# Sparse attention feeding a two-layer network: the scores of two head pairs in one visit to half-height products

## The chip, the cores and the metric

The kernel runs on one core of one Trainium2 chip. The metric is device time in microseconds (us), the median of several executions. The core has TensorE (PE, with its weight loads as PEld), VectorE (DVE), ScalarE (ACT), GpSimd (POOL) and SyncE (SP, here only a queue of DMAs). TensorE writes to PSUM[...].

## The reference

Eight batches (b) of eight heads, 576 positions, head size 64. Heads 0 to 3 see the last 32 positions, heads 4 to 7 the earlier positions of the same residue modulo 32. Then a two-layer network on all 4608 positions, with 512 inputs, 2048 hidden units and a PReLU between.

```python
scores = scale * np.matmul(q, k.transpose(0, 1, 3, 2))
mask_local = (rel >= 0) & (rel < 32)
mask_strided = (rel >= 0) & (pos[None, :] % 32 == pos[:, None] % 32)
attn = softmax(np.where(mask, scores, -1e9))          # local for heads 0-3, strided for 4-7
x = np.matmul(attn, v).transpose(0, 2, 1, 3).reshape(4608, 512)
h = x @ w_in
out = (np.maximum(h, 0.0) + alpha * np.minimum(h, 0.0)) @ w_out
```

## The kernel before, in words

**Network.** It works in nine blocks n of 512 positions, each in 30 steps i. Steps 0 to 15 are the first layer (`lin1_piece`): one step makes 128 hidden units for 512 positions with four products of 512 columns (line L678; eight of 256 in block 4, whose positions wrap in the ring `xT`) into one of three PSUM banks hb0 to hb2, handed out in turn by `hbank()`. ACT makes `neg` from the bank (L697), then DVE makes `gT` from `neg` and the bank (L700), which frees the bank. Steps 16 to 29 are the second layer (`lin2_sums`): seven products of half-size matrices in place of eight, two steps each, eight products of 256 columns a step (L811), into three accumulators A, B and C in the same three banks. The seven products need sums of parts of `gT` (`g_sum`, L760): on POOL at steps 5, 9 and 13, the rest on DVE at steps 16, 18 and 20. Accumulator C is written first at step 26.

**Attention.** It is cut into pieces that stand in one list, and each step of the network takes its share (`attn_n`, `attn_step`), so that block n carries batch n+1. A head pair is g = 4b + hp; hp 0 and 1 are local, 2 and 3 strided. Two pairs make a unit u = g // 2. The pieces of a pair are:

- Scores ("S", `score_both`). For each of 6 groups of 96 queries (local) or 8 groups of 72 (strided) and each of two heads y, a product of half height: the 64 rows of head y, rows 0-63 or 64-127 of the array, so that two heads' products stand side by side. A visit is one such run of products. The first half of the pair's groups goes to a two-bank PSUM tile `sp`, the other half to two tiles `sph` of the `ps` pool. ACT takes the exponential into an SBUF tile `et` (one for `sp`, L464; one for each `sph`, L474), and POOL multiplies with the mask (L468, L470, L477). The exps of the `sph` tiles wait in a list `defer`, of which each `attn_step` runs one.
- Attention times v ("P", `pv_piece`): products of 65 columns into a `ps` tile `pv` (L512; six products, or four in the third piece of a strided pair, PV(4) below), then a reciprocal (L521) and a multiply (L523) on DVE, which free it.
- Transposes of the result into `xT`: by DMA on SP (`x_dma`, with `x_copy` on ACT), or for hp 3 on PE ("X", `xp`).

The `ps` pool has three one-bank buffers, used in rotation by `sph`, `pv`, `xp` and the transposed inputs. Every engine works in the order written (`keep`); `late` puts L700 behind PE's next piece. POOL's queue also issues loads (`load_d`, `load_v`, `load_l`), SP's the transposing DMAs (`transpose_d`, `transpose_l`) and the stores.

The order of the pieces is:

```python
if okA:
    seq.append(("S", lambda a=a: score_both(pairs[a])))
if okP:
    seq.append(("P", Pv(p, 0)))
...
if 8 <= g - 2 < npair and not pairs[g - 2].xd:
    seq.append(("X", X(g - 2)))
if okP:
    seq.append(("P", Pv(p, 1)))
```

Of the kernel before, what the change touches and what calls it, by code (L numbers as in the profile page):

```python
# [9 lines left out]
F32 = mybir.dt.float32  # L10
# [22 lines left out]
def kernel(  # L33
# [10 lines left out]
    nc = tc.nc  # L44
# [56 lines left out]
    vss = [cpool.tile([128, 4, 8, 65], F16, name=f"vs{i}") for i in range(2)]  # L101
    ets = [cpool.tile([128, 800], F16, name=f"et{i}") for i in range(NE)]
    x16s = cpool.tile([80, 1024], F16)
# [57 lines left out]
    def cast_s(b, nm, eng):  # L161
        t16 = hpool.tile([128, 2, 512], F16, tag=f"{nm}s", bufs=2, name=f"{nm}s")
# [77 lines left out]
    def make_pair(g):  # L240
# [14 lines left out]
        P.pgroups = ([0, 1, 2], [3, 4, 5], [6, 7]) if P.strided else P.sgroups  # L255
        if P.lx:
            P.sgroups = ([0, 1, 2, 3], [4, 5])
        P.et = {}
# [163 lines left out]

    defer, defer_et = [], {}
    late = []
    second = {"on": False}

    def score_both(P):

        w, r = P.w, 72 if P.strided else 128
        for i in range(2):  # L430
# [9 lines left out]
            for x, t in enumerate(grp):  # L440
                if P.dx:
                    q0 = k0 = 80 * (4 * (2 * P.pr + t % 2) + t // 2)
                elif P.lx:
                    j = 3 * (2 * P.pr + t % 2) + t // 2
                    q0, k0 = 96 * j, 128 * j
                else:
                    q0, k0 = w * t, 32 + 72 * t if P.strided else 96 * t
                for y in range(2):
# [4 lines left out]
                        skip_group_check=True))  # L453
                    P.et[(2 * (t // 2) + y, t % 2) if P.dx or P.lx else (t, y)] = (et, n * y + w * x)
            ev = et[0:r, 0 : 2 * n]
            if not P.strided and i == 0 and not P.lx:
                mv = ev.rearrange("r (y c) -> r y c", y=2)
                m = mfirst.unsqueeze(1).to_broadcast([r, 2, n])
            else:
                z = 2 * w if P.lx and i == 0 else 0  # L460
                mv = ev[:, z:].rearrange("r (c f) -> r c f", f=w)
                m = (mstr if P.strided else mother).unsqueeze(1).to_broadcast([r, (2 * n - z) // w, w])
            if i == 0:
                keep(nc.scalar.activation(  # L464
                    ev.rearrange("r (y c) -> r y c", y=2), sp[0:r, :, 0:n], AF.Exp, scale=SCALE))
                if P.lx:
                    fv = ev[:, 0 : 2 * w].rearrange("r (c f) -> r c f", f=w)
                    keep(nc.gpsimd.tensor_tensor(  # L468
                        fv, fv, mfirst[:, 0:96].unsqueeze(1).to_broadcast([r, 2, w]), op=ALU.mult))
                keep(nc.gpsimd.tensor_tensor(mv, mv, m, op=ALU.mult))  # L470
                continue
# [6 lines left out]

            defer_et["et"] = et
            if second["on"]:  # L480
                ex(0)
                defer.append(lambda: ex(1))
            else:
                defer.extend([lambda: ex(0), lambda: ex(1)])

    def pv_piece(P, a):
        run_masks(P)
        while defer and any(P.et[z][0] is defer_et["et"] for z in P.et):
            defer.pop(0)()
        if P.x16 is None:  # L490
# [86 lines left out]
    for g in range(7, npair + 2):  # L577
# [6 lines left out]
        seq = []  # L584
        if okA:
            seq.append(("S", lambda a=a: score_both(pairs[a])))
# [66 lines left out]
    def attn_step(end):  # L653
# [6 lines left out]
        if defer:  # L660
            defer.pop(0)()

# [98 lines left out]

    lay, held = {}, {}

# [214 lines left out]
    for m in (2, 1, 0, *range(3, 16)):  # L978
# [97 lines left out]
```

## Time and profile before

| what | value |
|---|---|
| median of 3 runs | 300.24 us (299.53 to 300.42) |
| the profiled execution | 300.0 us, of which the span 298.1 us |
| PE, DVE, ACT, POOL busy in the span | 289.9, 227.8, 173.5, 168.5 us |
| blocks 3, 4 and 5, from first layer to first layer | 122.8 to 153.0, to 183.3, to 213.5 us: 30.2 each |
| in block 5 (183.3 to 213.5): PE, DVE, ACT, POOL busy | 30.1, 23.6, 18.2, 20.0 us |
| L678, a product of 512 columns | 0.379 us from start to end, one every 0.216 |
| L811, a product of 256 columns | 0.273 us, one every 0.109 |
| L697 on ACT, L700 on DVE | 0.597 and 0.744 us |
| granted clock | 1.0 throughout |

A row of the timeline has the start in us from the span's start, the duration of the row, engine, line, operation, output and inputs, the shapes, how many instructions are merged in it, and in brackets how long the engine was idle before it and what ended the wait. A PE row ends with its last result, some 0.16 us after the next product can start.

### The profile page before, as it was taken

Reading aid. Unit: us, or ns where it says so; the run is one execution under the profiler, and the core shown is the slowest. Engines: PE = TensorE matmul, PEld = TensorE weight load, DVE = VectorE, ACT = ScalarE, POOL = GpSimd, SP = SyncE. Lnnn points to the kernel's source line nnn. Section 1 sums busy time; section 2 is a strip of 40 time slices with the busy share of each in tenths; the row PEclk is TensorE's granted clock in tenths of the full one; section 3 lists DMA queues with packets and bytes.
Section 4 is the critical chain, followed back from the end, with each engine's and each line's share of the span. In section 5 each row is a group of like instructions: output and inputs, shape, how many; then the busy total and the mean of one; then the engine's idle time right before and its main releaser. Section 6 shows DMA issues by size and latency. Waiting matters only on the chain.

```text
span 298.1 us, 7107 instructions
## 1 busy us (share of the span) xinstructions
PE 289.9 (97%) x2808; PEld 193.6 (65%) x2808; DVE 227.8 (76%) x427; ACT 173.5 (58%) x325; POOL 168.5 (57%) x182
## 2 busy tenths in 40 slices
PE   7899998999999999999999999999999999999995
PEld 3664445644886478646898887468746864784584
DVE  5788868979975988488848894889488858946872
ACT  3566556888557773776377636763676257406620
POOL 8952289359757996777777778665555003101300
PEclk9999999999999999999999999999999999999999
DMA  7999999995998969999999999993811140022004
GB/s 219 204 202 207 205 238 266 170 175 178 177 154 186 111 100 127 173 192 160 132 209 177 138 141 182 184 144 54 201 22 21 24 141 0 2 71 73 0 2 141
DMA packets 102273, 41.01 MB, mean 138 GB/s; under 512 B 80720, under 2 KB 99424, under 8 KB 102240
## 3 DMA queue, kind: packets, MB, share of 16 engines
q0 software_dynamic: 56336, 19.25, 61.1%
q1 hardware_dynamic: 45632, 20.78, 35.3%
q10 hardware_dynamic: 272, 0.52, 0.6%
q8 instruction: 22, 0.36, 0.6%
q14 instruction: 11, 0.09, 0.1%
HBM read 38.60 MB, written 9.44 MB: 161 GB/s over the span
## 4 chain that ended last, share of the span: by engine, by line
PE 80%; DMA 11%; POOL 4%; issue 2%; DVE 2%; ACT 1%; POOLq 0%
PE hb L678 36%; PE hb L811 32%; DMA ks<-in_k_dram 6%; PE pv L512 4%; DMA win<-in_moe_w_in_dram 3%; PE sp L450 2%; DMA ql<-in_q_dram 2%; PE hb L715 2%; PE opl L811 1%; PE xp L533 1%; PE tp L280 1%; DVE gT L700 1%; PE sph L450 1%; POOL ql L217 1%; POOL vl L205 0%
## 5 line engine op out<-in xcount | busy, mean ns | idle before, releaser
L678 PE MATMUL hb<-xT,win 128*128 128x512 f16 (+1 forms) x616 | 127.2, 357 | 0.0
L700 DVE SCALAR_TENSOR_TENSOR gT<-neg,oma,hb 128x512 f16<-128x512 f32 x138 | 100.7, 744 | 33.0 <-ACT neg L697 26.3
L697 ACT ACTIVATE neg<-hb 128x512 f32<-128x512 f32 x138 | 82.1, 597 | 32.7 <-PE hb L678 31.5
L678 PEld LDWEIGHTS <-win 128*128 128x128 f16 x640 | 60.0, 98 | 53.8
L760 POOL TENSOR_TENSOR gsum<-gT 128x512 f16<-128x512 f16 x23 | 26.5, 1152 | 68.9 <-DVE gT L700 68.9
L811 PEld LDWEIGHTS <-gsum 128*128 128x128 f16 x512 | 47.3, 98 | 6.0 <-DVE gsum L760 0.5
L811 PEld LDWEIGHTS <-gT 128*128 128x128 f16 x384 | 35.9, 98 | 6.0 <-issue 0.5
L470 POOL TENSOR_TENSOR et<-et,mmul 128x576 f16<-128x576 f16 (+1 forms) x24 | 30.6, 1274 | 14.6 <-issue 7.8
L823 ACT COPY o<-hb 128x512 f32<-128x512 f32 (+1 forms) x32 | 18.1, 569 | 32.5 <-PE hb L811 32.5
L523 DVE TENSOR_TENSOR x<-pv,rc 96x384 f16<-96x384 f32 (+2 forms) x65 | 34.5, 531 | 2.2
L811 PE MATMUL hb<-wout,gT 128*128 128x256 f16 x248 | 30.8, 273 | 0.1
L811 PE MATMUL hb<-wout,gsum 128*128 128x256 f16 x248 | 30.5, 272 | 0.0
L811 PE MATMUL hb<-wsum,gsum 128*128 128x256 f16 x248 | 30.3, 273 | 0.0
L477 POOL TENSOR_TENSOR et<-et,mmul 72x576 f16<-72x576 f16 (+2 forms) x24 | 29.3, 1220 | 0.4 <-ACT et L474 0.4
L826 DVE TENSOR_TENSOR o<-hb,o 128x512 f32<-128x512 f32 (+1 forms) x24 | 16.3, 681 | 17.0 <-PE hb L811 12.5
L464 ACT ACTIVATE et<-sp 72x576 f16<-72x576 f32 (+2 forms) x24 | 16.4, 685 | 20.6 <-PE sph L450 17.2
L512 PEld LDWEIGHTS <-et 72*128 72x128 f16 (+1 forms) x416 | 21.9, 98 | 8.0 <-issue 1.3
L474 ACT ACTIVATE et<-sph 72x288 f16<-72x288 f32 (+2 forms) x48 | 17.8, 388 | 0.0
L521 DVE RECIPROCAL rc<-pv 72x6 f32<-72x6 f32 (+2 forms) x80 | 14.5, 181 | 2.9 <-PE pv L512 2.4
L715 PE MATMUL hb<-wout,gT 128*128 128x512 f16 x64 | 15.6, 379 | 0.2 <-ACT osb L720 0.2
L811 PE MATMUL hb<-wsum,gT 128*128 128x256 f16 x120 | 15.3, 273 | 0.0
L760 DVE TENSOR_TENSOR gsum<-gT 128x512 f16<-128x512 f16 (+2 forms) x17 | 14.7, 865 | 0.2
(117 smaller groups left out, 318.0 us busy)
## 6 DMA issues: line engine op xcount, KB each, us to landing
out_dram<-o SPq DMA_DIRECT2D x31, 256.0 KB, 3.1
stv<-in_v_dram POOLq DMA_DIRECT2D x8, 288.0 KB, 8.4
vl<-in_v_dram POOLq DMA_DIRECT2D x6, 384.0 KB, 9.3
wout<-in_moe_w_out_dram POOLq DMA_DIRECT2D x4, 512.0 KB, 16.9
qsd<-in_q_dram POOLq DMA_DIRECT2D x6, 288.0 KB, 7.6
ksd<-in_k_dram POOLq DMA_DIRECT2D x6, 288.0 KB, 7.1
kl<-in_k_dram SPq DMA_DIRECT2D x3, 512.0 KB, 5.1
ql<-in_q_dram POOLq DMA_DIRECT2D x3, 512.0 KB, 6.4
```

The source lines that it names most:

```text
L470: keep(nc.gpsimd.tensor_tensor(mv, mv, m, op=ALU.mult))
L474: keep(nc.scalar.activation(ev[:, n * y : n * y + n], sps[y][0:r, 0:n], AF.Exp, scale=SCALE))
L477: keep(nc.gpsimd.tensor_tensor(mv, mv, m, op=ALU.mult))
L512: keep(nc.tensor.matmul(pv[:, 65 * x : 65 * x + 65], et[0:r, c : c + 128], v16[0:r, 2 * P.pr + hh, t, :] if P.strided else v16[:, 6 * (2 * ...
L523: keep(nc.vector.tensor_tensor(P.x16[0:w, c0 : c0 + 64 * nb].rearrange("r (c e) -> r c e", e=64), pvv[:, :, 0:64], rc[0:w, 0:nb].unsqueeze ...
L678: keep(nc.tensor.matmul(hps[:, dst : dst + w], win16[:, kk, 128 * m : 128 * m + 128], xT[:, kk, src : src + w], start=(first and kk == kks ...
L697: keep(nc.scalar.activation(neg, hps, AF.Relu, scale=-1.0))
L700: keep(nc.vector.scalar_tensor_tensor(gTs[n][:, m, :], neg, oma[:, m : m + 1], hps, op0=ALU.mult, op1=ALU.add))
L715: keep(nc.tensor.matmul(ops, gTs[n][:, kf, 128 * mt : 128 * mt + 128], wout16[:, kf, :], start=(kf == 0), stop=(kf == 15)))
L760: keep(eng.tensor_tensor(o[:, k0:k1], x[:, k0:k1], y[:, k0:k1], op=op))
L811: keep(nc.tensor.matmul(dst, lhs[:, kf, 128 * mt : 128 * mt + 128], rhs[:, kf, :], start=(first and own and kf == 0), stop=(kf == 7), skip ...
L823: keep(nc.scalar.copy(o, x))
```

## The change

From g = 16 on (batch 4) the first pair of a unit makes the scores of both pairs in one visit (`score_unit`), with the same products in another order. For each head y one stream runs through: the first pair's groups but the last one or ones, into `sp`; the leftover groups of both pairs, into c3 (y = 0, a `ps` tile) or c4 (y = 1); the second pair's groups, into c1 or c2 (`ps` tiles). c4 is an hb bank: the next in turn in the first layer, accumulator C's in the second. The exps of c4 and `sp` run in the visit; that of c3 does too in the second layer, and is first in `defer` in the first layer; c1 and c2 follow in `defer`. The results lie in `evs` (two tiles e1 and e2 for each of two units) and in `ets` for the leftovers (e3), and the masks are cut differently. The visit of a strided unit stands after the first PV piece of its slot, that of a local unit after the second; empty pieces "N" hold a place in the list and issue nothing of their own. The first batches' casts of strided q and k lie in `evs` now.

```diff
+    evs = [[cpool.tile([128, 1088], F16, name=f"ev{i}{j}") for j in range(2)] for i in range(2)]
...
-            t16 = hpool.tile([128, 2, 512], F16, tag=f"{nm}s", bufs=2, name=f"{nm}s")
+            t16 = evs[b]["qk".index(nm)][:, 0:1024].rearrange("p (f c) -> p f c", f=2)
...
+    def score_unit(u):
+        A, Bp = pairs[2 * u], pairs[2 * u + 1]
+        w, r, nb = A.w, 72 if A.strided else 128, 7 if A.strided else 5
+        n = nb * w
+        (e1, e2), e3 = evs[u % 2], ets[u % 2]
+        sp = pbpool.tile([128, 2, 512], F32, tag="sp", name="sp")
+        c3, c1, c2 = [pspool.tile([128, 512], F32, tag="ps", name="sph") for _ in range(3)]
+        c4 = lay["Cf"] if second["on"] else hbank()
+        rest = [(A, nb), (Bp, nb)]
+        streams = [
+            [(A, s, sp[:, 0], w * s) for s in range(nb)]
+            + [(P, s, c3, w * z) for z, (P, s) in enumerate(rest)]
+            + [(Bp, s, c1, w * s) for s in range(nb)],
+            [(A, s, sp[:, 1], w * s) for s in range(nb)]
+            + [(P, s, c4, w * z) for z, (P, s) in enumerate(rest)]
+            + [(Bp, s, c2, w * s) for s in range(nb)],
+        ]
+        for x in range(2 * nb + 2):
+            for y in range(2):
+                P, s, o, c = streams[y][x]
...
+                keep(nc.tensor.matmul(
+                    o[:, c : c + w], P.kT[hf, k0 : k0 + 128], P.qT[hf, q0 : q0 + w],
+                    start=(c == 0), stop=(c == (1 if s == nb else nb - 1) * w), skip_group_check=True))
...
+        def ex3():
+            ev = e3[0:r, 0 : 4 * w]
+            ex(ev[:, 0 : 2 * w], c3[0:r, 0 : 2 * w])
+            mask(ev.rearrange("r (c f) -> r c f", f=w),
+                 (mstr if A.strided else mother).unsqueeze(1).to_broadcast([r, 4, w]))
+        def ex2():
+            ex(e2[0:r, n : 2 * n], c2[0:r, 0:n])
+            masks(e2)
+        ex(e3[0:r, 2 * w : 4 * w], c4[0:r, 0 : 2 * w])
+        ex(e1[0:r, 0 : 2 * n].rearrange("r (y c) -> r y c", y=2), sp[0:r, :, 0:n])
+        masks(e1)
+        if second["on"]:
+            ex3()
+        else:
+            defer.append(((e3,), ex3))
+        defer.append(((e2,), lambda: ex(e2[0:r, 0:n], c1[0:r, 0:n])))
+        defer.append(((e2,), ex2))
...
+        units = g >= 4 * (DX + 2)
+        visit = okA and units and a % 2 == 0
-        if okA:
+        if okA and not units:
             seq.append(("S", lambda a=a: score_both(pairs[a])))
...
+        if visit and g % 4 == 2:
+            seq.append(("S", lambda a=a: score_unit(a // 2)))
+            seq.append(("N", lambda: None))
         if okP:
             seq.append(("P", Pv(p, 1)))
+        if visit and g % 4 == 0:
+            seq.append(("N", lambda: None))
+            seq.append(("S", lambda a=a: score_unit(a // 2)))
+            seq.append(("N", lambda: None))
...
-            for t in ets:
-                keep(nc.gpsimd.memset(t[:, 640:800], 0.0))
+            for t in evs[0] + evs[1]:
+                keep(nc.gpsimd.memset(t[:, 1024:1088], 0.0))
```

More of the change, by code (lines that the diff above doesn't have):

```diff
@@ L101 @@
     vss = [cpool.tile([128, 4, 8, 65], F16, name=f"vs{i}") for i in range(2)]
-    ets = [cpool.tile([128, 800], F16, name=f"et{i}") for i in range(NE)]
+    ets = [cpool.tile([128, 640], F16, name=f"et{i}") for i in range(NE)]
+    evs = [[cpool.tile([128, 1088], F16, name=f"ev{i}{j}") for j in range(2)] for i in range(2)]
     x16s = cpool.tile([80, 1024], F16)
@@ L161, in cast_s @@
     def cast_s(b, nm, eng):
-        t16 = hpool.tile([128, 2, 512], F16, tag=f"{nm}s", bufs=2, name=f"{nm}s")
+        t16 = evs[b]["qk".index(nm)][:, 0:1024].rearrange("p (f c) -> p f c", f=2)
         if eng[0] == eng[1]:
@@ L255, in make_pair @@
         P.pgroups = ([0, 1, 2], [3, 4, 5], [6, 7]) if P.strided else P.sgroups
-        if P.lx:
-            P.sgroups = ([0, 1, 2, 3], [4, 5])
         P.et = {}
@@ L421, in score_piece, with mask, masks, ex @@
         keep(nc.gpsimd.tensor_tensor(ev, ev, m, op=ALU.mult))
-    defer, defer_et = [], {}
+    defer = []
     late = []
+    lay = {}
     second = {"on": False}
+    def score_unit(u):
[18 more added lines that the diff above has]
+                P, s, o, c = streams[y][x]
+                if P.dx:
+                    q0 = k0 = 80 * (4 * (2 * P.pr + s % 2) + s // 2)
+                elif P.lx:
+                    j = 3 * (2 * P.pr + s % 2) + s // 2
+                    q0, k0 = 96 * j, 128 * j
+                else:
+                    q0, k0 = w * s, 96 * s
+                hf = slice(64 * y, 64 * y + 64)
+                keep(nc.tensor.matmul(
+                    o[:, c : c + w], P.kT[hf, k0 : k0 + 128], P.qT[hf, q0 : q0 + w],
+                    start=(c == 0), stop=(c == (1 if s == nb else nb - 1) * w), skip_group_check=True))
+                key = (2 * (s // 2) + y, s % 2) if P.dx or P.lx else (s, y)
+                P.et[key] = (e3, 2 * w * y + c) if s == nb else (e1 if P is A else e2, n * y + c)
+        def mask(v, m):
+            keep(nc.gpsimd.tensor_tensor(v, v, m, op=ALU.mult))
+        def masks(e):
+            ev = e[0:r, 0 : 2 * n]
+            if A.lx:
+                fv = ev[:, 0 : 2 * w].rearrange("r (c f) -> r c f", f=w)
+                mask(fv, mfirst[:, 0:96].unsqueeze(1).to_broadcast([r, 2, w]))
+                fv = ev[:, 2 * w :].rearrange("r (c f) -> r c f", f=w)
+                mask(fv, mother.unsqueeze(1).to_broadcast([r, 2 * nb - 2, w]))
+                return
+            k = 4 if A.strided else 3
+            fv = ev.rearrange("r (y c) -> r y c", y=2)
+            if A.strided:
+                m = mstr
+                for lo, hi in ((0, k), (k, nb)):
+                    mask(fv[:, :, w * lo : w * hi].rearrange("r y (c f) -> r y c f", f=w),
+                         m.unsqueeze(1).unsqueeze(1).to_broadcast([r, 2, hi - lo, w]))
+            else:
+                mask(fv[:, :, 0 : w * k], mfirst.unsqueeze(1).to_broadcast([r, 2, w * k]))
+                mask(fv[:, :, w * k :].rearrange("r y (c f) -> r y c f", f=w),
+                     mother.unsqueeze(1).unsqueeze(1).to_broadcast([r, 2, nb - k, w]))
+        def ex(o, i):
+            keep(nc.scalar.activation(o, i, AF.Exp, scale=SCALE))
+        def ex3():
[11 more added lines that the diff above has]
+            ex3()
+        else:
+            defer.append(((e3,), ex3))
+        defer.append(((e2,), lambda: ex(e2[0:r, 0:n], c1[0:r, 0:n])))
+        defer.append(((e2,), ex2))
@@ L442, in score_both @@
                     q0 = k0 = 80 * (4 * (2 * P.pr + t % 2) + t // 2)
-                elif P.lx:
-                    j = 3 * (2 * P.pr + t % 2) + t // 2
-                    q0, k0 = 96 * j, 128 * j
                 else:
@@ L453, in score_both @@
                         skip_group_check=True))
-                    P.et[(2 * (t // 2) + y, t % 2) if P.dx or P.lx else (t, y)] = (et, n * y + w * x)
+                    P.et[(2 * (t // 2) + y, t % 2) if P.dx else (t, y)] = (et, n * y + w * x)
             ev = et[0:r, 0 : 2 * n]
-            if not P.strided and i == 0 and not P.lx:
+            if not P.strided and i == 0:
                 mv = ev.rearrange("r (y c) -> r y c", y=2)
@@ L459, in score_both @@
             else:
-                z = 2 * w if P.lx and i == 0 else 0
-                mv = ev[:, z:].rearrange("r (c f) -> r c f", f=w)
-                m = (mstr if P.strided else mother).unsqueeze(1).to_broadcast([r, (2 * n - z) // w, w])
+                mv = ev.rearrange("r (c f) -> r c f", f=w)
+                m = (mstr if P.strided else mother).unsqueeze(1).to_broadcast([r, 2 * n // w, w])
             if i == 0:
@@ L465, in score_both @@
                     ev.rearrange("r (y c) -> r y c", y=2), sp[0:r, :, 0:n], AF.Exp, scale=SCALE))
[L466 to L469, printed above, removed]
                 keep(nc.gpsimd.tensor_tensor(mv, mv, m, op=ALU.mult))
@@ L477, in ex @@
                     keep(nc.gpsimd.tensor_tensor(mv, mv, m, op=ALU.mult))
-            defer_et["et"] = et
             if second["on"]:
                 ex(0)
-                defer.append(lambda: ex(1))
             else:
-                defer.extend([lambda: ex(0), lambda: ex(1)])
+                defer.append(((et,), lambda: ex(0)))
+            defer.append(((et,), lambda: ex(1)))
     def pv_piece(P, a):
         run_masks(P)
-        while defer and any(P.et[z][0] is defer_et["et"] for z in P.et):
-            defer.pop(0)()
+        used = [P.et[t, y][0] for t in P.pgroups[a] for y in range(2)]
+        while any(e is z for es, _ in defer for e in es for z in used):
+            defer.pop(0)[1]()
         if P.x16 is None:
@@ L660, in attn_step @@
         if defer:
-            defer.pop(0)()
+            defer.pop(0)[1]()
     gTs = {}
@@ L760, in g_sum @@
         keep(eng.tensor_tensor(o[:, k0:k1], x[:, k0:k1], y[:, k0:k1], op=op))
-    lay, held = {}, {}
+    held = {}
     def store(n, i, j, osb, mts=(0, 1)):
```

## The prediction

> **What bounds the kernel now.** First the page: busy shares, then the chain of waits.
>
> ```profile
> PE 289.9 (97%) x2808; PEld 193.6 (65%) x2808; DVE 227.8 (76%) x427; ACT 173.5 (58%) x325; POOL 168.5 (57%) x182
> ...
> PE 80%; DMA 11%; POOL 4%; issue 2%; DVE 2%; ACT 1%; POOLq 0%
> ```
>
> PE is the bound and the chain runs along it, so in the changed stretch (blocks 2 to 6, about 105 to 240 us) what PE saves or waits for counts one to one. The question is where PE leaves its own pace. The timeline of block 5's first layer:
>
> ```profile
> 186.07 2.75 PE L678 MATMUL hb<-xT,win 128*128 128x512 f16 x12
> ...
> 187.44 0.18 DVE L521 RECIPROCAL rc<-pv 96x6 f32<-96x6 f32 x1
> 187.66 0.55 DVE L523 TENSOR_TENSOR x<-pv,rc 96x384 f16<-96x384 f32 x1
> ...
> 188.13 2.10 DVE L700 SCALAR_TENSOR_TENSOR gT<-neg,oma,hb 128x512 f16<-128x512 f32 x3
> ...
> 188.76 0.30 PE L450 MATMUL sp<-qT,kT 64*128 64x72 f16 x8
> ...
> 188.89 0.29 PE L450 MATMUL sph<-qT,kT 64*128 64x72 f16 x8
> ...
> 189.12 2.76 PE L678 MATMUL hb<-xT,win 128*128 128x512 f16 x12
> ```
>
> *The visit.* Twelve products of 0.216 from 186.07 should end at 188.66; the first score product starts 0.10 later. Four pairs take 0.13 (sp to sph), so eight take 0.26, but L678 returns 0.36 after the start: another 0.10. A visit costs 0.46 us, 0.20 of it fixed.
>
> *The bank.* Step 3 starts at 186.07; PE takes 1.03 to its last result (L678 x4 at 225.72), ACT's neg 0.60, DVE's L700 0.745, hand-overs some 0.12: 2.50 us until its hb bank is free. Three steps of 0.865 are 2.60. So a bank comes back 0.1 us early if DVE and ACT are idle. DVE isn't after a PV piece: reciprocal and multiply put 0.69 (187.44 to 188.13) ahead of the next L700. Step 3's L700 ended at 188.87 (188.13 + 0.745), and only the score visit made the next user of its bank wait until 189.12.
>
> The second layer of the same block:
>
> ```profile
> 201.74 1.91 PE L811 MATMUL hb<-wsum,gsum 128*128 128x256 f16 x16
> ...
> 203.16 1.21 DVE L760 TENSOR_TENSOR gsum<-gT,gsum 128x2048 f16<-128x2048 f16 x1
> 203.58 0.28 PEld L450 LDWEIGHTS <-kT 64*128 64x128 f16 x12 [0.21 <-issue]
> 203.58 0.34 PE L450 MATMUL sp<-qT,kT 64*128 64x96 f16 x8
> 203.76 0.25 PE L450 MATMUL sph<-qT,kT 64*128 64x96 f16 x4
> 203.94 0.77 PEld L811 LDWEIGHTS <-gsum 128*128 128x128 f16 x8
> 203.94 1.05 PE L811 MATMUL hb<-wsum,gsum 128*128 128x256 f16 x8
> ...
> 204.50 0.42 DVE L523 TENSOR_TENSOR x16s<-pv,rc 72x256 f16<-72x256 f32 x1
> ...
> 205.07 0.34 PE L512 MATMUL pv<-vs,et 72*128 72x65 f16 x6
> ```
>
> Eight products of 0.109 from 203.94 end at 204.82, but PV starts at 205.07: 0.24 lost. Two sph tiles and the last pv tile fill the ps pool's three buffers; the oldest is free when L523 ends at 204.92, and PE starts 0.15 later. DVE was late because L760 (1.21) stood ahead. The same gap follows the score visits at 143.1 and 173.4.
>
> **What the skill says.** "TensorEngine Tiling (Array Packing)", Key Properties: changing the tiling mode drains TensorE. The trace agrees: 0.10 us at each edge of a visit. "TensorE: Matmul & The Clock Gate", Part 3, The mechanism: tiles in different row groups overlap. Agrees: a pair of 72-column products takes 33 ns, one 65-column PV product 30. "Perfetto Trace Analysis", Optimization Strategy: a gap that repeats can mean too few PSUM buffers. Agrees: the 0.24 us above. Same page, Optimizing Scalar/DVE Operations: half of an instruction's profiled latency can overlap the next. Here part of it does: starts stand 0.08 to 0.11 closer than durations, so I use such pitches (neg 0.49, L700 0.70).
>
> **The change, part by part.** The order of the changed program's instructions, step by step in blocks 3 to 5: steps 0-2, PV, 3-5, PV, 6-7, visit, 8-12, PV, 13-15, PV; second layer 1 step, PV, 2, PV(4), 1, PV, 1, PV, 3, visit, 2, PV(4), 2, PV, 1, xp, 1. The one visit per layer serves two pairs. I lay block 5's measured times on this order.
>
> 1. *Visits.* PE's score products stay the same in number and size; sixteen visits become eight. Saved: 8 x 0.21 = **-1.7**.
>
> 2. *The old ps wait.* PV no longer follows the visit with only one step between. Saved: 3 x 0.24 = **-0.7**.
>
> 3. *First layer, steps 6 and 8.* PV now stands where the first visit stood (0.18 for 0.46), so step 6 comes at 188.85 and its bank at 188.92: 0.07. That second PV puts its 0.69 ahead of step 6's L700, which ends at 191.60. The visit takes the third hb bank for c4, so step 8 needs step 6's bank, at 188.92 + 0.87 + 0.87 + 0.10 + 0.63 = 191.38. Wait: 191.65 - 191.38 = 0.27. ACT meets c4 (0.28), sp (1008 columns, 0.99 by the slope between 0.638 for 576 and 0.811 for 768), and c3 (0.28) at once, 1.2 with overlap after neg of step 7 at 190.86, free at 192.6, just as step 8 ends (192.68). c1 and c2 (0.58 each) then push neg of steps 9 and 10 by 0.1 and 0.2; the bank for step 12 is then exactly due: 0.03. Sum 0.37, in four blocks: **+1.5**.
>
> 4. *Second-layer visit.* PV at the layer boundary puts 0.69 on DVE between the last L700 and L760's first sum. That alone costs little: the products that need that sum come late in step 18 (in block 6 of before, which has such a PV, PE waits 0.07). But it stays in DVE's queue. With X the start of step 15, DVE runs L700 to X+2.44, PV 0.69, L760 0.34 + 1.28, PV 0.69, L760 1.13, PV(4) 0.55, PV 0.69, L760 1.13, PV: its multiply ends at X+9.56. PE by its own pace starts the visit at X+8.81 and reaches c2 at X+9.12, and c2 is the third ps tile, so it needs that last pv tile. Before, two ps tiles per visit left the newest alone. Wait: 9.56 + 0.15 - 9.12 = 0.59, in blocks 3, 4 and 5: **+1.8**. Block 2 has different spacing (transposes, no boundary PV): DVE ends 0.4 ahead, no wait.
>
> 5. *Block 6* has the boundary PV two steps after another: step 13 and the first sum some 0.1 later each: **+0.2**.
>
> 6. *Covered or equal.* ACT: five exps a unit for six, 2.8 us for 2.9. POOL's masks: 5.3 us a unit either way; e1's two in the second layer (1.74 to 3.9 after the visit's start) are needed at 4.2, slack 0.3. In the first layer POOL then has e1 (2.27), e3 (0.7), gsum (1.15), e2 (2.27), now ahead of load_d's two issues (1.5), and gsum of step 13 (1.15): ends near 201.6 where PE wants it at 201.3. That 0.3 is inside the 0.59 of item 4, since PE late there is PE less late at c2; if that cover goes, it counts. DMA transposes on SP move from a score piece to the PV piece at the same place; their users are over 3 us off. x_copy on ACT moves behind c2, nobody waits there. Shared buffers for the first casts and four memsets for six change no order elsewhere.
>
> Sum: -1.7 - 0.7 + 1.5 + 1.8 + 0.2 = **+1.1 us**. The profiled execution took 300.0 (span 298.1), which gives 301.1; the median 300.24 stands 0.2 above it, so I predict **301.3 us**.
>
> Unknown sizes: the masks with two broadcast dimensions (72x2x288, 72x2x216) are in no row. Nearest are 1.27 and about 1.0 for 576 and 432 elements. A gain has no reason that I see; slower by a half is the other end. An exp of 960 or 1008 columns is extrapolated: 0.95 to 1.1. PE's wait for a bank: 0.05 after one semaphore (194.65 to 194.70), 0.15 after two.
>
> **Rivals.**
> *The visits' saving stays (faster).* DVE's queue is the mechanism, in two places: step 8 and c2. If DVE recovers earlier than laid out (pitches shorter when it works without a break), the waits go and items 1 and 2 remain: 300.24 - 2.4 = 297.8. For it: the saving reads alike at every visit of the timeline. Against it: step 8's bank is short even with DVE idle (2.46 us for a chain of 2.50). It decides below 1.5 us of new waits in all.
> *POOL becomes late.* If the new masks cost 30% more, the four in each first layer add 1.4 us ahead of gsum of step 13; its cover is 0.3, and L760's second sum waits for it too. Some 0.8 net in three blocks: 301.3 + 2.4 = 303.7. For it: nine us of POOL work in a row from 192.7. Against it: POOL's share over block 5 is only 20 of 30 us.
> *Nothing measurable.* Waits at half my size: +1.6 against -2.4, 299.5. This lies between the first two and is how the forecast would shade into no change.
>
> **How the numbers follow.** My forecast as laid out has a chance of 0.50 (300.2 to 302.3), the saving 0.22 (297.7 to 299.9, the halved waits in it), POOL 0.28 (302.3 to 304.5). A measurement of this kernel tells 0.3%, 0.9 us, from no change (three runs spread 0.9). So faster 0.16 (most of the second), same 0.28 (0.22 of the first, 0.06 of the second), slower 0.56. Likeliest is slower, by a narrow margin, since +1.1 is close to 0.9. Range 298.6 to 304.0.
>
> **What would show it.** In the profile after: eight visits of 24 or 32 products, first to next L760 line about 0.63 us where nothing waits; a gap of about 0.27 before step 8's first product, released by L782; in the second-layer visits of blocks 3 to 5 a gap of about 0.5 inside the visit, before its second sph tile, released by L596; no 0.24 before PV after the visit. Wrong if those gaps are under 0.1, if the released-by engine is POOL or ACT, or if the gaps sum to over 5 us.

## The result, and the profile after

The changed kernel takes **306.9 us** (306.73 to 307.1, 4 runs) against 299.88 us for the kernel before (299.49 to 300.42, 4 runs, beside it): ratio 1.0233, 95% interval 1.0212 to 1.0254. The prediction had the direction right and the size wrong: 301.3 was forecast, and 306.9 lies above its range. The profiled execution took 306.88 us, its span 305.1 us; before it was 300.0 and 298.1, so 7.0 us of span have to be found. In six of the experiments below (e2, e6, e8, e9, e13, e14; in none of the others) some executions, 15 of 35 in all, took several us longer than the fastest; the ratios leave these out, and readings come from profiles of the other executions.

The page of the changed kernel, busy shares and the chain of waits:

```profile
PE 290.7 (95%) x2808; PEld 194.1 (64%) x2808; DVE 232.2 (76%) x427; ACT 173.2 (57%) x317; POOL 173.7 (57%) x182
...
PE 55%; DVE 15%; DMA 13%; POOL 7%; issue 4%; ACT 3%; ACTq 0%; POOLq 0%
```

PE has the same work and the same busy time as before (0.8 us more). But the chain now runs along PE for 55% of the span and no longer 80%: DVE has 15% of it where it had 2. And two engines got *busier* with the same number of instructions: DVE by 4.4 us, POOL by 5.2. The groups of the page (line, engine, operation, tiles, count, then busy us, mean ns of one, idle before and its releaser) say which:

```profile
L893 PE MATMUL hb<-wsum,gsum 128*128 128x256 f16 x248 | 32.2, 273 | 3.7 <-POOL gsum L842 2.0
...
L218 POOL COPY vs<-stv 72x1024 f16<-72x1024 f16 x12 | 18.6, 1578 | 3.6 <-DMA stv<-in_v_dram 3.6
L842 DVE TENSOR_TENSOR gsum<-gT 128x512 f16<-128x512 f16 (+2 forms) x17 | 18.2, 1074 | 0.1
```

In the kernel before the same DVE sums took 865 ns on average and POOL's copies of v 1031 ns. PE waits 3.7 us ahead of the products with `wsum` and `gsum` (0.0 before), 2.0 of it for a POOL sum.

The first-layer visit, in the timeline of block 5, is as laid out:

```profile
194.72 0.40 PE L456 MATMUL sp<-qT,kT 64*128 64x72 f16 x14
...
195.02 0.39 PE L456 MATMUL sph<-qT,kT 64*128 64x72 f16 x14
...
195.62 2.75 PE L760 MATMUL hb<-xT,win 128*128 128x512 f16 x12 [0.20 <-DVE gT L782]
```

From the last score product to the next network product PE takes 0.39 us, where 0.13 is its pace: 0.26 of waiting, released by L782, as predicted. So is the wait for c2 in the second-layer visit, here in block 4:

```profile
179.18 1.21 DVE L842 TENSOR_TENSOR gsum<-gT 128x2048 f16<-128x2048 f16 x1
...
180.24 0.39 PE L456 MATMUL sp<-qT,kT 64*128 64x96 f16 x10
...
180.53 0.55 DVE L596 TENSOR_TENSOR x<-pv,rc 72x384 f16<-72x384 f32 x1
...
181.14 0.38 PE L456 MATMUL sph<-qT,kT 64*128 64x96 f16 x9 [0.40 <-DVE x L596]
```

PE starts the visit at 180.24 and could have gone on to c2 at 180.59; the multiply ends at 181.08, and c2 starts at 181.14. What the prediction doesn't have is step 18. Block 5, from POOL's second load issue to the second half of step 18:

```profile
203.76 0.71 POOL L134 DMA_DIRECT2D ksd<-in_k_dram  x1
...
204.50 1.16 POOL L842 TENSOR_TENSOR gsum<-gT 128x512 f16<-128x512 f16 x1
...
204.88 0.60 PE L893 MATMUL hb<-wsum,gsum 128*128 128x256 f16 x4
204.94 1.98 DVE L842 TENSOR_TENSOR gsum<-gT 128x512 f16<-128x512 f16 x1
...
205.60 2.22 POOL L218 COPY vs<-stv 72x1024 f16<-72x1024 f16 x2
205.72 0.39 PE L893 MATMUL hb<-wsum,gsum 128*128 128x256 f16 x2 [0.23 <-POOL gsum L842]
206.85 2.12 DVE L842 TENSOR_TENSOR gsum<-gsum,gT 128x1024 f16<-128x1024 f16 x2
206.98 0.39 PE L893 MATMUL hb<-wsum,gsum 128*128 128x256 f16 x2 [0.87 <-DVE gsum L842]
```

Step 18 needs POOL's sum of step 13 and then DVE's first sum. POOL's ends at 205.66. DVE's, 0.41 us when alone, starts at 204.94 and takes 1.98. PE's wait (start to start, less its pace of 0.11) is 0.40 and 1.04 us. In the same way PE waits 0.38 and 0.95 in block 4, and 1.70 in block 3, where POOL's sum was the one that took longer:

```profile
140.40 2.47 POOL L842 TENSOR_TENSOR gsum<-gT 128x512 f16<-128x512 f16 x1
```

Read off the same way, all that PE gained and lost against the kernel before:

| what | predicted, us | profile after, us |
|---|---|---|
| eight visits for sixteen | -1.7 | -1.7 |
| old ps wait | -0.7 | -0.7 |
| first layer, steps 6, 8, 12 (four blocks) | +1.5 | +1.6 (step 8: 0.27 each; step 6: 0.05 to 0.08; step 12: 0.06 to 0.16, none in block 4) |
| c2 in the second-layer visits of blocks 3, 4, 5 | +1.8 | +2.0 (0.55, 0.55, 0.86) |
| block 6 | +0.2 | +0.1 |
| step 18 in blocks 3, 4, 5 | 0 ("covered") | **+4.5** |
| steps 20 to 22 of block 5; step 0 of block 3; sums in block 2 | 0 | +0.5; +0.3; +0.4 |
| sum | +1.1 | +7.0 |

### The profile page after: what moved, and what is told of

Same layout as the page of the kernel before. It is cut to its first block, busy times and chain, and to the rows that moved or that the text cites. A ratio compares the mean times of both kernels' runs of the same rounds, so it can differ in the third digit from the quotient of the medians.

```text
span 305.1 us, 7072 instructions
## 1 busy us (share of the span) xinstructions
PE 290.7 (95%) x2808; PEld 194.1 (64%) x2808; DVE 232.2 (76%) x427; ACT 173.2 (57%) x317; POOL 173.7 (57%) x182
## 4 chain that ended last, share of the span: by engine, by line
PE 55%; DVE 15%; DMA 13%; POOL 7%; issue 4%; ACT 3%; ACTq 0%; POOLq 0%
PE hb L760 27%; PE hb L893 20%; DMA ev<-in_k_dram 6%; DVE gsum L842 6%; DVE gT L782 4%; DMA win<-in_moe_w_in_dram 3%; DMA xs<-x16s 3%; DVE x L596 3%; PE pv L585 2%; DVE x16s L596 2%; DMA ql<-in_q_dram 2%; PE hb L797 2%; ACT neg L779 2%; POOL ev L463 1%; POOL gsum L842 1%
## 5 line engine op out<-in xcount | busy, mean ns | idle before, releaser
L782 DVE SCALAR_TENSOR_TENSOR gT<-neg,oma,hb 128x512 f16<-128x512 f32 x138 | 100.5, 744 | 33.8 <-ACT neg L779 28.1
L760 PEld LDWEIGHTS <-win 128*128 128x128 f16 x640 | 60.7, 98 | 55.6 <-issue 1.9
L842 POOL TENSOR_TENSOR gsum<-gT 128x512 f16<-128x512 f16 x23 | 27.8, 1211 | 63.6 <-DVE gT L782 53.1
L463 POOL TENSOR_TENSOR ev<-ev,mmul 72x576 f16<-72x576 f16 (+5 forms) x32 | 35.3, 1111 | 18.8 <-ACT ev L486 17.9
L893 PE MATMUL hb<-wsum,gsum 128*128 128x256 f16 x248 | 32.2, 273 | 3.7 <-POOL gsum L842 2.0
L893 PE MATMUL hb<-wout,gsum 128*128 128x256 f16 x248 | 29.8, 273 | 0.0
L218 POOL COPY vs<-stv 72x1024 f16<-72x1024 f16 x12 | 18.6, 1578 | 3.6 <-DMA stv<-in_v_dram 3.6
L842 DVE TENSOR_TENSOR gsum<-gT 128x512 f16<-128x512 f16 (+2 forms) x17 | 18.2, 1074 | 0.1
L543 POOL TENSOR_TENSOR et<-et,mmul 128x576 f16<-128x576 f16 (+1 forms) x8 | 10.2, 1279 | 11.8 <-issue 7.9
L585 PEld LDWEIGHTS <-et 128*128 128x128 f16 (+1 forms) x224 | 12.3, 98 | 4.4 <-DVE x16s L596 0.3
L585 PEld LDWEIGHTS <-ev 72*128 72x128 f16 (+1 forms) x192 | 11.4, 98 | 3.7 <-DVE x16s L596 0.4
```

Of the source, the lines that this page charges most:

```text
L218: keep(nc.gpsimd.tensor_copy(o, i))
L463: keep(nc.gpsimd.tensor_tensor(v, v, m, op=ALU.mult))
L585: keep(nc.tensor.matmul(pv[:, 65 * x : 65 * x + 65], et[0:r, c : c + 128], v16[0:r, 2 * P.pr + hh, t, :] if P.strided else v16[:, 6 * (2 * ...
L760: keep(nc.tensor.matmul(hps[:, dst : dst + w], win16[:, kk, 128 * m : 128 * m + 128], xT[:, kk, src : src + w], start=(first and kk == kks ...
L782: keep(nc.vector.scalar_tensor_tensor(gTs[n][:, m, :], neg, oma[:, m : m + 1], hps, op0=ALU.mult, op1=ALU.add))
L842: keep(eng.tensor_tensor(o[:, k0:k1], x[:, k0:k1], y[:, k0:k1], op=op))
```

## The experiments

**Theories.** *A*: POOL's queue order. In the changed kernel the loads and the copies of v are no longer behind a visit's masks, so POOL works beside DVE's second-layer sums, and POOL and DVE shut each other out. *B*: the PV piece at the layer boundary (item 4 of the prediction) makes DVE late, and POOL's part follows from that. *C*: the visits' own shape costs the time; clear one wait and another comes.

| kernel | span, us | ratio to the kernel before (95%) |
|---|---|---|
| before; after | 298.1; 305.1 | 1; 1.0233 (1.0212 to 1.0254) |
| e1_load_early | 305.4 | 1.0204 (1.0169 to 1.0238) |
| e2_pool_clear | 302.1 | 1.0143 (1.0083 to 1.0203) |
| e3_no_edge_pv | 306.5 | 1.0303 (1.0258 to 1.0347) |
| e4_before_mask_again | 301.1 | 1.0114 (1.006 to 1.0168) |
| e5_pool_clear_loads_early | 309.1 | 1.0292 (1.025 to 1.0333) |
| e6_and_second_visit_late | 306.0 | 1.0099 (1.0067 to 1.0132) |
| e7_and_first_visit_late | 308.0 | 1.0311 (1.027 to 1.0352) |
| e8_copies_late_only | 302.0 | 1.0078 (1.0042 to 1.0113) |
| e9_transposes_early | 298.6 | 1.0037 (1.0017 to 1.0057) |
| e10_and_third_sum_late | 301.5 | 1.0127 (1.01 to 1.0153) |
| e11_copies_alone | 303.8 | 1.0179 (1.0155 to 1.0203) |
| e12_before_third_sum_late | 297.7 | 0.9987 (0.9969 to 1.0005) |
| e13_sum_late_loads_ahead | 307.8 | 1.029 (1.0251 to 1.033) |
| e14_loads_ahead | not read | 1.0218 (1.016 to 1.0276) |
| e15_after_third_sum_late | 304.5 | 1.0206 (1.0189 to 1.0223) |

A span is that of one profiled execution, and one wait in it varies without any edit: in block 2, where POOL's sum meets DVE's as well, PE loses 0.57 us in after and 0.78 in e15, 0.14 in e9 and 1.09 in e10, two pairs whose programs are the same up to there. So a difference of 1 us between two spans says little, and the waits at each place are compared instead. The expectations of e1 to e4 are in times of whole executions, which are 1.8 us above the span; the later ones are in spans.

### Do DVE and POOL shut each other out? (e4_before_mask_again)

The kernel before, with one more POOL multiply (the last strided mask again, which changes no value) beside DVE's first sums:

```diff
+                    again[:] = [lambda: keep(nc.gpsimd.tensor_tensor(mv, mv, m, op=ALU.mult))]
+                    again[0]()
...
                 lin2_sums(n, i - 16)
+                if n in (3, 4, 5) and i == 16:
+                    again[0]()
```

> The kernel before, with the last mask multiply of the strided pair done a second time on POOL at step 16 of blocks 3, 4 and 5 (a mask of zeros and ones, so the values stay), about 1.27 us at the moment when DVE runs its sums L760 and POOL was idle. If POOL and DVE shut each other out there, L760's sums (1.29 us for two) stretch by about 1 us, and the PV piece that waited 0.24 waits longer: 301 to 303. If they don't, 299.9 and L760 as before.

The span grew by 3.0 us. The timeline of the kernel before at this place, a load issue on POOL beside the sums:

```profile
139.76 0.42 DVE L760 TENSOR_TENSOR gsum<-gT 128x512 f16<-128x512 f16 x1
139.83 1.24 POOL L142 DMA_DIRECT2D qx<-in_q_dram  x1
...
140.10 1.28 DVE L760 TENSOR_TENSOR gsum<-gsum,gT 128x1024 f16<-128x1024 f16 x2
```

and of the kernel with the mask once more:

```profile
139.72 1.36 POOL L477 TENSOR_TENSOR et<-et,mmul 72x576 f16<-72x576 f16 x1
...
139.87 2.37 DVE L761 TENSOR_TENSOR gsum<-gsum,gT 128x1024 f16<-128x1024 f16 x2
...
143.68 0.26 PE L450 MATMUL sph<-qT,kT 64*128 64x96 f16 x3 [0.42 <-DVE x16s L524]
...
145.44 0.22 PE L513 MATMUL pv<-vs,et 72*128 72x65 f16 x2 [0.53 <-DVE x16s L524]
```

The two sums take 2.37 us for 1.28, while the load issue had left them at their length. DVE stays late, and three steps later PE waits inside the visit (0.42) and ahead of PV (0.70 by starts, 0.24 before). So one POOL multiply of 1.36 us, on an engine that had only load issues there, costs about 1 us a block. The Trainium skill says this, on the page "SBUF — State Buffer", section "SBUF: two separate sides": an instruction of DVE with two SBUF inputs and an instruction of GpSimd that reads SBUF lock the same port pair for their whole length, and "the other fully blocks". The runs agree in size, and in that DVE's L782, with one input in PSUM, keeps its 744 ns in both kernels. That the pair goes to whoever starts first is not how the records read: in block 3 of after POOL's sum starts 0.45 ahead of DVE's and loses, in blocks 4 and 5 it starts 0.48 and 0.44 ahead and wins.

### Which of POOL's work is in the way? (e1_load_early, e11_copies_alone, e2_pool_clear, e8_copies_late_only)

Three moves: `load_d` ahead of the first-layer visit; the copies of v behind the second-layer visit; `load_l` there too.

```diff
-                    if g % 4 == 2 and DX <= c and c + 1 < B:
-                        load_d(c + 1)
...
+                if (first if units else lastp) and g % 4 == 2 and DX <= c and c + 1 < B:
+                    load_d(c + 1)
```
```diff
+        at_s = [i for i, z in enumerate(seq) if z[0] == "S"]
+        if visit and g % 4 == 0:
+            nslots = [i for i in nslots if i > at_s[0]]
```

e1 has the first move:

> The changed kernel with load_d (two loads, 1.5 us of POOL's queue) moved from the last PV piece of its slot to the first, ahead of the visit, where POOL is idle. Theory A (POOL's queue): gsum of step 13 is late behind e2's masks and load_d, and whatever POOL runs next collides with DVE's sums L842. Then gsum comes 1.5 us earlier and PE's first wait in step 18 (0.4) goes, but the next loads or copies move up beside L842, which stays slow: 303.5 to 305.5. Theory B (the PV at the layer boundary holds DVE's sums back by 0.69): the sums are as late as before, 306.5 to 307.

e11 has the second:

> After with nothing but the v copies (and the load behind them) behind the second-layer visit; load_d stays between the visit's last mask and POOL's sum. It asks how much of the 4.5 us each of the two moves takes away. load_d puts 1.5 us of POOL ahead of the sum, so the sum ends about 0.4 after step 18 wants it, and DVE's first sum stands beside it: 0.4 + 0.5 a block if the two sums shut each other out for the length of POOL's only; 1.3 a block as in after if the load issued next also counts. So span 301.8 to 303.5, against 302.0 with both moves in e8_copies_late_only (1.9 to 2.9 of it waits for transposes, which should not be here as load_d comes after the transposes).

e8 has both:

> e1_load_early and the v copies (with the load behind them) behind the second-layer visit, load_l left where it was (behind step 18 to 20). It parts copies from load issues. If the copies are what stretches DVE's sums, the sums are back to 0.4 to 0.7 each and the span is close to that of e5_pool_clear_loads_early (within 0.7). If the issue of load_l on POOL's queue (1.2 and 1.4 us[...]) stretches them as the copies do, one or two sums of each block take over 1.4 us and 0.5 to 1.0 us a block stay: span 301 to 302.5.

e2 has both, and `load_l` behind the visit:

> As the one before, and also the copies of v (L218 before) and the loads of q and k (load_l) moved behind the local unit's visit, so that POOL has nothing to run between gsum of step 13 and the masks of the visit in step 23. Theory A: L842's first sum is back at 0.43 us, all waits in step 18 (4.5 us over blocks 3 to 5) go: 302.4, with the waits for c2 (0.55 each) still there. Theory B: no more than 1 us, 306.

PE's waits for the sums of steps 18 to 20 in blocks 3, 4, 5 add up to 4.6 us in after (1.70, 1.33, 1.59), 2.3 in e1 (1.09, 1.07, 0.14), 3.8 in e11 (1.69, 0.44, 1.69) and nothing in e8 and e2: neither move does it alone. In e1 POOL's sum is early, but DVE's second and third sum still take 1.52 us each for 0.68, in the timeline of block 3:

```profile
142.30 1.44 POOL L143 DMA_DIRECT2D kx<-in_k_dram  x1
142.47 2.96 DVE L842 TENSOR_TENSOR gsum<-gsum,gT 128x1024 f16<-128x1024 f16 x2
...
143.74 2.59 POOL L218 COPY vs<-stv 72x1024 f16<-72x1024 f16 x2
...
145.49 0.28 PE L893 MATMUL hb<-wsum,gsum 128*128 128x256 f16 x1 [0.83 <-DVE gsum L842]
```

The third sum stands beside the copies, the second almost wholly beside the load issue ahead of them. c2 waits 0.86 in all three blocks, other waits behind the late sums grow by 0.8 and block 2's by as much, and its span is that of after. By its time, 306.8 us, e1 would speak for B, which expected 306.5 to 307; but POOL's sum comes earlier and the waits at steps 18 to 20 are halved, as A alone expected. In e11, whose span is 0.3 us above the range expected, the sum of step 13 still meets DVE's first sum, and POOL loses in blocks 3 and 5 (2.45 and 2.47 us for 1.15).

In e8 `load_l` issues right beside the sums, which stay at 0.41 and 1.28 for two: an issue by itself does no harm, copies, masks and sums do. With the copies behind it in POOL's queue an issue is another matter. Block 4 of after, where they come at 176.40, and of e11, where they and the load behind them come behind the visit:

```profile
173.12 1.87 DVE L842 TENSOR_TENSOR gsum<-gT 128x512 f16<-128x512 f16 x1
173.74 1.23 POOL L143 DMA_DIRECT2D qx<-in_q_dram  x1
```
```profile
173.97 0.98 DVE L845 TENSOR_TENSOR gsum<-gT 128x512 f16<-128x512 f16 x1
174.59 1.23 POOL L143 DMA_DIRECT2D qx<-in_q_dram  x1
```

DVE's sum, held up by POOL's in both, ends 1.18 us after that one in after and 0.29 in e11. In block 3 a DVE sum beside the same issue takes 1.38 us in after and 0.69 in e11. So the copies cost DVE time before their own record begins, as far as these pairs show; how they do it stays open.

e2 and e8 have the step-18 waits gone, but their spans are still 4 us longer than before (by the ratios 1.4 and 0.8%), and e2's 303.9 us are 1.5 more than A expected. The second-layer visits now wait for a transpose on SP's queue; in e2, block 3:

```profile
137.41 6.49 SPq L153 DMA_TRANSPOSE kT<-kx  x1
...
147.41 0.39 PE L456 MATMUL sp<-qT,kT 64*128 64x96 f16 x10 [1.27 <-DMA kT<-kx]
```

It took 1.80 us in after. With `load_d` ahead of the visit its transfers and these transposes are in flight together. The waits add to 4.7 us in e2 (1.34, 2.26, 1.14) and 2.7 in e8 (0.97, 1.72), and hide the wait for c2 there.

### The boundary PV (e3_no_edge_pv)

```diff
-            cnt = int(acc)
+            cnt = int(acc) if i != 15 or n < 3 else 0
```

> The changed kernel with no attention piece after step 15 in blocks 3 on, so that the PV piece at the layer boundary comes one step later and DVE's first sum runs ahead of its division; POOL's queue as it was. Theory B: the waits in step 18 go, 302.4. Theory A: POOL's gsum of step 13 is as late as before, so PE's first wait stays; DVE's sum starts 0.7 earlier and may or may not meet POOL: 304 to 306.5. The wait for c2 stays in both.

The span grew to 306.5, and the median of 309.2 us is above what either theory expected. DVE's first sum is at its own length (0.43), but POOL's sum is as late as before, the next sums meet POOL all the same, and PV waits more, in block 4 of e3:

```profile
173.27 3.10 DVE L842 TENSOR_TENSOR gsum<-gsum,gT 128x1024 f16<-128x1024 f16 x2
...
177.12 0.36 PE L585 MATMUL pv<-vs,ev 72*128 72x65 f16 x6 [1.10 <-DVE x16s L596]
```

B falls.

### Transfers in order (e5_pool_clear_loads_early, e9_transposes_early)

Two ways to give the transposes room: `load_l` a whole block earlier (e5, on e8), or `transpose_l` some five steps earlier (e9, on e8).

```diff
-                if i_last and g % 4 == 3 and LX <= c + 2 < B:
+                if g % 4 == (3 if g < 16 else 1) and (i_last if g < 16 else lastp) and LX <= c + 2 < B:
```
```diff
-                if first and g % 4 == 2 and LX <= c + 1 < B:
+                if first and g % 4 == 1 and LX <= c + 1 < B:
                     transpose_l(c + 1)
```

> After with three moves of POOL's work: load_d ahead of the first-layer visit, the v copies (and the load behind them) behind the second-layer visit, and load_l two batches ahead at the block's first steps, where its transfers have a whole block to land. Theory A (POOL's queue order: loads and copies that run while DVE makes the second layer's sums): the step-18 waits (4.5 us in after) are gone, and so are the 1.34, 2.26 and 1.14 us that the second-layer visits of e2_pool_clear waited for the transpose of kx, which came from load_l issued only 10 us ahead. What returns is the wait of c2 for the last PV tile's multiply, 0.59 in each of three visits, which in e2_pool_clear lay beside the wait for the transpose: span 302.1 - 4.7 + 1.8 = 299.2 (298.5 to 300.0), about 0.4% slower than before. Theory C (the visits' own shape costs the time, the POOL order only moves it): the second-layer visit finds another wait of 1 us or more, span 302 or above.

> e8_copies_late_only, and the transposes of kx and qx issued at a block's first piece instead of some five steps later, so that they no longer stand beside load_d's transfers. In e8_copies_late_only the transpose of kx took 8.5 and 9.6 us instead of the 2.9 to 3.9 of after, SP's queue behind it was late, and two second-layer visits waited 0.97 and 1.72 us for a transpose; one step-0 product waited 0.22. Theory A with its sequel (after POOL, the DMA queues are next): these 2.9 us go and nothing takes their place: span 302.0 - 2.9 = 299.1, with the waits of the two other visits back at 0.5 each where the transpose had hidden them: 299.1 + 1.0 = 300.1 at most. Theory C (something always waits here): a wait of the same size appears elsewhere and the span stays at 302.

e5 was a miss: six loads within 7 us of a block's start, the transposes of kx behind them (7.03 us in the median, 1.80 to 3.89 in after), and one visit that waits 8.7 us for it. In blocks 3 and 5 it does show what was expected: no wait at step 18, c2 waiting 0.44.

e9 is the kernel that A calls for. Its page and groups:

```profile
PE 289.4 (97%) x2808; PEld 195.1 (65%) x2808; DVE 226.8 (76%) x427; ACT 173.3 (58%) x317; POOL 165.9 (56%) x182
...
L896 PE MATMUL hb<-wsum,gsum 128*128 128x256 f16 x248 | 30.9, 272 | 0.0
...
L218 POOL COPY vs<-stv 72x1024 f16<-72x1024 f16 x12 | 12.2, 1031 | 3.2 <-DMA stv<-in_v_dram 3.2
L845 DVE TENSOR_TENSOR gsum<-gT 128x512 f16<-128x512 f16 (+2 forms) x17 | 14.6, 859 | 0.1
```

POOL has lost 7.8 busy us against after and DVE 5.4, with the same instructions. Block 4 of its timeline:

```profile
168.53 1.15 POOL L845 TENSOR_TENSOR gsum<-gT 128x512 f16<-128x512 f16 x1
...
169.62 1.25 POOL L143 DMA_DIRECT2D qx<-in_q_dram  x1
...
170.44 1.04 PE L896 MATMUL hb<-wsum,gsum 128*128 128x256 f16 x8
170.51 0.41 DVE L845 TENSOR_TENSOR gsum<-gT 128x512 f16<-128x512 f16 x1
170.84 1.28 DVE L845 TENSOR_TENSOR gsum<-gsum,gT 128x1024 f16<-128x1024 f16 x2
```

The span is 298.6, in the fastest of its executions, 6.5 us less than after with the same visits. From one first-layer visit to the next are 30.4 us (129.84, 160.25, 190.65); the kernel before has 30.2 a block. What is left of a block is the prediction's own sum: -0.42 for two visits, -0.24 for the ps wait, 0.27 + 0.07 + 0.04 in the first layer, 0.44 for c2: +0.16. C falls: with POOL and the transfers in order, nothing waits but what the prediction had named.

### The visits a step later (e6_and_second_visit_late, e7_and_first_visit_late)

On e5, an empty piece moved from behind a visit to ahead of it, for the second layer (e6) or the first (e7):

```diff
-            seq.append(("N", lambda: None))
-            seq.append(("S", lambda a=a: score_unit(a // 2)))
-            seq.append(("N", lambda: None))
+            seq += [("N", lambda: None)] * 2
+            seq.append(("S", lambda a=a: score_unit(a // 2)))
```

> e5_pool_clear_loads_early, and the second-layer visit one step later (the empty piece that stood behind it now stands ahead). If c2 waits for the multiply of the last PV tile, as the prediction said, the multiply is done a step earlier than needed and the 0.59 goes in three visits: 1.8 us less than e5_pool_clear_loads_early, span about 297.5. Against it: the PV piece that follows comes one step after the visit instead of two, and its first product may wait for a bank that the visit's exponentials hold: if so, a wait of 0.3 to 1 us appears there and the gain is under 1 us.

> e5_pool_clear_loads_early, and the first-layer visit one step later (step 8; the empty piece now stands ahead). The prediction laid 0.27 in each of four blocks to the network product behind the visit waiting for a bank that DVE empties late since PV's multiply (0.69) runs ahead of it. One step later that multiply is through: 4 x 0.25 = 1.0 us less than e5_pool_clear_loads_early. Rival: the wait comes from c4 taking the third bank alone, whatever DVE does: then it stays at 0.27 in the step behind the visit and the span is the same within 0.3. The PV piece behind the visit comes one step earlier after it and may wait for the masks: then slower.

Both waits went where they were expected to go: c2 waits nothing in e6, and behind the first-layer visit of e7 0.04 is left of the 0.27. Neither is seen to gain. In e6 step 24, now ahead of the visit, waits 0.2 for DVE's third sum, and the PV piece behind the visit waits 0.55, in each of blocks 3 to 5:

```profile
150.85 0.19 PE L585 MATMUL pv<-vs,ev 72*128 72x65 f16 x1 [0.39 <-ACT et L486]
```

In e7 POOL's masks are a step later as well: the first product behind the boundary's PV waits 0.2 and step 18 waits 0.44 in each block. The totals of both say little, since each also waits once for the transposed x (2.3 and 4.4 us), as e5 does for the transpose of kx.

### c2 and DVE's order (e10_and_third_sum_late, e15_after_third_sum_late, e12_before_third_sum_late, e13_sum_late_loads_ahead, e14_loads_ahead)

DVE's third sum (1.21, needed at step 24) behind the last PV tile's multiply and not ahead of it, on e9 (e10), on after (e15) and on the kernel before (e12):

```diff
-        elif i == (2 if quiet(n) else 4):
+        elif i == (2 if quiet(n) else 4 if n < 3 else 5):
```

> e9_transposes_early, and DVE's third sum (1.21, needed at step 24) issued at step 21 instead of step 20, so that it stands behind the last PV tile's multiply on DVE and not ahead of it. If c2 in the second-layer visit waits for that multiply because of DVE's order (item 4 of the prediction), the multiply ends some 1.2 us earlier and the 0.48 to 0.59 of each visit go: 1.4 to 1.8 us less than e9_transposes_early, span 297.5 to 298.5: about as fast as the kernel before or a little faster. If the bank itself is the limit (the exponentials and PV pieces hold all banks whatever DVE's order), c2's wait stays. If the sum comes too late at its new place, step 24's first product waits for it, up to 0.5.

> The changed kernel with DVE's third sum a step later and nothing else. If c2 waits because of DVE's order, the 0.55, 0.55 and 0.86 us of the three second-layer visits go and about 0.17 comes back behind each visit: 1.5 us less than after, span 303.6. The step-18 waits of 4.5 us stay. If the late sum brings a wait for xs (2.8 us in e10_and_third_sum_late), the span is 305 or more and a product of step 0 waits for it.

> The kernel before with DVE's third sum a step later. No visit waits for c2 there. If the late sum costs nothing by itself: span 298.1 within 0.3. If it delays step 24's product (by the 0.17 of e10_and_third_sum_late) in three blocks: 298.6. If it brings the wait for xs: 300 or more.

In e10 and e15 c2 doesn't wait any more, in any visit: that wait is DVE's order. In e10 step 24 waits 0.17 in its place, in e15, where DVE is later, 0.28, 0.29 and 0.59:

```profile
181.17 0.50 PE L893 MATMUL hb<-wout,gsum 128*128 128x256 f16 x3 [0.22 <-DVE gsum L842]
```

In the kernel before the move changes nothing that can be measured. But e10 is slower than e9, by 1.0 us in block 2, which the edit leaves alone, and by 2.7 us of waits for x at the starts of blocks 4, 5 and 6, the longest for the x of a strided pair:

```profile
153.99 1.30 ACT L627 COPY xT<-xs 128x576 f16<-128x576 f16 x1 [4.18 <-DMA xs<-x16s]
...
155.34 0.38 PE L763 MATMUL hb<-xT,win 128*128 128x256 f16 x2 [1.14 <-ACT xT L627]
```

The issues of loads around it, the last number being us from issue to landing (first e9, then e10):

```profile
kx<-in_k_dram POOLq DMA_DIRECT2D x1, 384.0 KB, 7.1
```
```profile
kx<-in_k_dram POOLq DMA_DIRECT2D x1, 384.0 KB, 16.7
```

With `load_l` a block ahead (the edit of e5), on e10 (e13) and on e9 (e14):

> e10_and_third_sum_late with load_l a whole block ahead, behind the other two loads of the block's first steps, so that no load is in flight while xs and the strided q and k are transposed at the block's end. If e10's new wait is load_l's transfer in the way of the xs transpose, it goes (2.8 us) and the c2 wait stays away: span 298.6 - 1.4 = 297.2, faster than the kernel before (298.1) by 0.3%. If the wait belongs to the later sum itself (the products of step 24 and what follows late), it stays at 2 us or more: span over 300. If the loads now pile up in the block's first half, the transposes of the strided q and k or the first-layer visit wait instead, and this run and e14_loads_ahead show the same loss.

> e9_transposes_early with load_l a whole block ahead, the third sum at its old place. Span 298.6 as e9_transposes_early if load_l's place doesn't matter there (its transfers were hidden), c2 waiting 0.5 in three visits. Over 299.5 if the loads pile up in the first half of the block.

Both were misses. The loads pile up in the block's first half, as in e5, and xs lands late (13.8 us in e13). In e13 step 0 and 1 of block 5 wait 1.4 and 5.0 us for x. So e10's late kx wasn't cured that way, and why kx took 16.7 us there with the order of loads that e9 has stays open; the late sum alone (e12, e15) doesn't bring a wait of that size.

No version with the new visits beats the kernel before. e9 beats the changed kernel and stays 0.2 to 0.6% slower than before.

## Why the prediction was wrong, point by point

**The bound and items 1 and 2** held: the visits save 0.21 each and the ps wait is gone.

**Item 3** held in place, releaser and size (0.27 at step 8, +1.6 for +1.5). e7 shows that the wait is PV's 0.69 ahead of L782 on DVE: a step later it is 0.04. The slope quoted for the exp of 1008 columns gives 1.03 us, not 0.99; it took 1.00, and nothing hung on it.

**Item 4** held: 0.55, 0.55 and 0.86 for 0.59 each, none in block 2 (0.04), and by the mechanism given (e10, e15). With POOL out of the way, as the prediction had laid it out, it is 0.44 (e9), so that the sum in after comes so near the forecast (+2.0 for +1.8) is in part luck. The terms listed for DVE's queue also add up to X+9.63, not X+9.56.

**Item 5** was +0.1 for +0.2.

**Item 6 is the step that failed**, in its sentence "That 0.3 is inside the 0.59 of item 4, since PE late there is PE less late at c2": step 18 was put at nothing in the sum, and its waits cost 4.5 us beside the full waits of item 4. POOL's end was laid out well, 201.6 for a sum that PE wants at 201.3; in the profile, some 4 us later in all, it is 205.66 for 205.32. Three things were wrong.

1. *Two durations that overlap were taken as if each were alone.* POOL's sum of 1.15 and DVE's first sum of 0.34 stood at the same time in the prediction's own layout. When they meet, either POOL's takes 2.47 (block 3) or DVE's takes 0.98 (e11, block 4), and 1.87 to 1.98 with the copies of v behind POOL's sum (blocks 4 and 5 of after). It could have been read before: in the kernel before, POOL's mask L468 takes 1.54 us at 204.91, beside DVE's sum at 204.84 (1.21 us), and 0.54 us at 210.50 with no sum beside it (the timeline of POOL):

```profile
204.91 1.54 POOL L468 TENSOR_TENSOR et<-et,mmul 128x192 f16<-128x192 f16 x1 [4.55 <-ACT et L464]
...
210.50 0.54 POOL L468 TENSOR_TENSOR et<-et,mmul 128x192 f16<-128x192 f16 x1
```

   There POOL lost and nobody waited.

2. *POOL's queue was followed to the sum of step 13 and no further.* Before, the copies of v stood behind the masks of a visit (208.52 in block 5). In the changed order no mask comes until step 23, so they run at 205.60, beside DVE's sums. e1 and e8, which differ by the place of these copies and of the load behind them, show what they cost: 2.3 us of waits at steps 18 to 20 against none. e11 shows that moving them is not enough: only block 4 gains (0.44 for 1.33), since POOL's sum still meets DVE's.

3. *A wait was said to lie inside a later one.* It moves DVE and PE by the same amount, so the c2 wait did not shrink: 0.55 to 0.86 are still there behind step 18's waits.

**Rivals.** The second named the right place, POOL's sum of step 13 and the DVE sum behind it, and the wrong cause: masks 30% dearer. They are not (2.35 us for two, priced at 2.27). Its price of 0.8 a block was 1.5. The remark that gaps that "sum to over 5 us" would make the forecast wrong describes what came.

## What to carry to other kernels

When a change moves work on POOL, lay POOL's instructions beside DVE's by time, not only each queue against its users: a sum of two SBUF tensors on DVE and a copy, sum or mask on POOL that overlap cost each other time (1.1 us for a mask of 1.36 in e4), and the mean duration of a group that changes with the same instructions shows it at once. Follow a queue past the instruction that looked critical to the next place where it blocks: here the copies behind the load issues cost DVE time even before they were seen to run. A wait that is said to be covered by a later one must be carried through every engine that sets the later one; if it delays them all alike, both waits are paid. And where loads have just enough room, moving one queue's order pushes the next: here POOL, then DMA, then DVE.

## What was not expected of the hardware

- A POOL load issue beside DVE's sums costs nothing (0.42 and 1.28 us in the kernel before, 0.41 and 1.28 in e9), a POOL multiply of 1.36 us costs 1.09. With copies of v behind the issue in POOL's queue, one DVE sum in each of blocks 3 and 4 takes 0.70 to 0.84 us longer beside the issue (after, e1, e3); with none there (the kernel before, e8, e9, e11) none takes over 0.02 longer. Why stays open.
- After a long wait PE runs at half pace. In e5, from 186.3 to 189.5, products of 256 columns came every 0.213 us in place of 0.109, after the wait of 8.7 us; the windows of its trace (stretch, its length, busy us and count of five engines, granted clock, DMA share, GB/s) show the clock:

```profile
185.00:189.60 4.60, 4.39 (x40) 3.31 (x41) 0.00 (x0) 2.34 (x5) 2.26 (x3) 0.50 0.99 93
189.60:194.00 4.40, 4.40 (x54) 3.85 (x53) 2.54 (x6) 2.03 (x3) 4.40 (x5) 1.00 0.55 88
```

  The Trainium skill describes it on "TensorE: Matmul & The Clock Gate", Part 1, What's actually happening: an idle window of some 3.4 us halves the clock until a busy one has passed. The half clock agrees, and so does the length where the waits were 8.7, 4.4 and 5.0 us (e5, e7, e13). But in e6 a wait of 2.33 us was enough, and in e2 one of 2.26 us was not. A wait for DMA that is near this length costs more than itself, which is part of why e5, e6, e7 and e13 are so far off.
